# A planned attention and rational-FFN kernel: the first batch's sixteen units in another order, and a planner that tries five slacks

## The chip, the core and the metric

One core of one Trainium2 chip runs the kernel. The metric is the device time of one execution in microseconds. The kernel before takes 781.16 us, the median of three runs (780.78 to 782.17).

## The reference

For each of 8 batches and 8 heads, 32 packed queries `p` attend over 576 keys and values of width 64; then the 576 queries `q` attend over the 32 packed rows that came out. The result, 4608 tokens of 512 features, goes through a feed-forward layer with a rational activation:

```
p_packed = sm_attn(p, k, v)
x = sm_attn(q, p_packed, p_packed)          # 4608 x 512
h = x @ w_in                                # 512 -> 2048
P = a[0] + a[1]*h + a[2]*h^2 + a[3]*h^3
Q = 1 + |b[0]|*|h| + |b[1]|*h^2
out = (P / (Q + 1e-6)) @ w_out              # 2048 -> 512
```

The weights arrive as 64-bit floats and are taken apart by integer instructions on the chip.

## The kernel before

A batch `bb` has 576 tokens in two halves `x` of 288; the 2048 hidden features are eight chunks `c` of 256. A **unit** is one (batch, half, chunk), 128 in all, and the list `units` (L950) gives their order: batch by batch, in each batch the first half's eight chunks and then the second half's.

A unit runs in `hidden` (L876). TensorE makes `h` for two sets of 128 features in the two PSUM tiles of `h_ring`, so the tile of a unit's first set comes free when ScalarE has read it three times (into `Y`, `U`, `sq`) and VectorE twice (the two instructions that write `Y` from `h`). GpSimd adds `U` and `sq`, ScalarE takes the logarithm and exponential into `V` (which is in PSUM), VectorE makes `Y`, `V` and the product `g`. Three steps later `acc_block` (L955) multiplies 256 of the unit's tokens by rows of `w_out` into two PSUM tiles of `acc_ring`; the eight chunks of one half add up there, then ScalarE copies the sum out. The 32 tokens of a half that are left over are collected in `G` and multiplied by `remainder`. `m_chunk` folds `w_in` into the packed rows, one tile `M[bb, c // 2]` for two chunks.

The weights of the first batch come in while it runs. There are 16 words to convert, eight chunks of `w_in` (`in`) and eight of `w_out` (`out`). `convert` issues for each word two ScalarE passes and three VectorE passes (`tensor_scalar`, `scalar_tensor_tensor`, `tensor_add` on integers; the third is a custom instruction in the trace and `ISA` in the built order). `due` (L430) says at which unit a word is wanted and sorts the list; a word of `in` is due two units ahead of its chunk, one of `out` three units behind. `DIVIDE` later splits each chunk of `w_out` in a high and a low part (ScalarE copy, GpSimd subtractions). The first `PLAIN` = 12 units multiply undivided.

None of this is the order on the chip. Every instruction is recorded by `Planner` (L32), and `order` (L249) lists them anew. `schedule` (L191) is a list scheduler with one queue per engine, costs per instruction and a way time between engines; `order` runs it forward and backward in turn and ranks by the backward run's times, `ROUNDS` = 8 rounds, and the plan with the earliest end is kept. `SLACK` = 150 ns is added to each way in the backward run. `shares` (L136) says which VectorE instructions can't run beside a GpSimd one: in the plan, one waits until the other is done. `tensor_scalar`, `tensor_copy` and the integer `tensor_add` are such, if nothing in PSUM takes part; the `scalar_tensor_tensor` of a conversion is not. Where the plan leaves TensorE idle in the first 150 us, `idle` puts in small multiplications by `zero` (L285).

Of the kernel before, what the change touches and what calls it, by code (L numbers as in the profile page):

```python
# [31 lines left out]
class Planner:  # L32
# [8 lines left out]
    TRANSPOSE, F32 = (15, 0.734), (30, 1.62)  # L41
# [15 lines left out]
    WAY.update({("sync", x): 80 for x in ENGINES})  # L57
    PASS = 200
    FIRST = {"tensor": 700.0, "vector": 800.0, "scalar": 2000.0, "gpsimd": 1400.0, "sync": 700.0}
    ROUNDS = 8  # L60
    SWITCH = 95
    SLACK = 150
    IN_FLIGHT = 8
    DMA_ISSUE, DMA_START, DMA_END = 420, 1400, 1200

# [70 lines left out]
    def shares(self, engine, calls):  # L136

        if engine == "gpsimd":
            return True
        if engine != "vector":  # L140
            return False
        name, args, _ = calls[0]
        aps = [x for x in args if isinstance(x, bass.AP)]
        if any(x.space == PSUM for x in aps):
            return False
        return name in ("tensor_scalar", "tensor_copy") or (name == "tensor_add" and aps[0].dtype == I32)

    def mode(self, engine, calls):

# [38 lines left out]
            edges.append(before)  # L188
        return edges

    def schedule(self, before, after, rank, back=False):  # L191

        n = len(rank)
        need = [len(x) for x in before]
        at, start, end = [0.0] * n, [0.0] * n, [0.0] * n
        soon = {e: [] for e in self.ENGINES}
        ready = {e: [] for e in self.ENGINES}
        free = dict.fromkeys(self.ENGINES, 0.0) if back else dict(self.FIRST)
        port = {"vector": 0.0, "gpsimd": 0.0}
        mode, landed, dma = None, [], 0.0  # L200
        for i in range(n):
            if not need[i]:
                heapq.heappush(soon[self.ops[i][0]], (0.0, rank[i], i))
        now = 0.0
        left = n
        while left:
            for e in self.ENGINES:
                while soon[e] and soon[e][0][0] <= now:
                    heapq.heappush(ready[e], heapq.heappop(soon[e])[1:])
                if free[e] > now or not ready[e]:  # L210
                    continue
                if e == "sync" and not back and len(landed) >= self.IN_FLIGHT and landed[-self.IN_FLIGHT] > now:
                    free[e] = landed[-self.IN_FLIGHT]
                    continue
                _, i = heapq.heappop(ready[e])
                left -= 1
                s = now
                if e == "tensor" and not back and self.modes[i] != mode:
                    s += self.SWITCH
                    mode = self.modes[i]  # L220
                if not back and self.shared[i]:
                    s = max(s, port["vector" if e == "gpsimd" else "gpsimd"])
                    port[e] = s + self.costs[i]
                start[i] = s
                end[i] = free[e] = s + self.costs[i]
                if e == "sync":
                    if back:
                        dma = max(dma, end[i]) + self.transfers[i]
                        end[i] = dma + self.DMA_START + self.DMA_END - self.DMA_ISSUE
                    else:  # L230
                        dma = max(dma, s + self.DMA_START) + self.transfers[i]
                        end[i] = dma + self.DMA_END
                        landed.append(end[i])
                for j in after[i]:
                    need[j] -= 1
                    f = self.ops[j][0]
                    way = self.WAY.get((f, e) if back else (e, f), self.PASS)
                    way += self.SLACK * (back and way > 0)
                    at[j] = max(at[j], end[i] + way)
                    if not need[j]:  # L240
                        heapq.heappush(soon[f], (at[j], rank[j], j))
            now = min(
                t
                for e in self.ENGINES
                for t in ([free[e]] if ready[e] else [max(soon[e][0][0], free[e])] if soon[e] else [1e12])
            )
        return start, end

    def order(self):  # L249
        n = len(self.ops)  # L250
        self.costs = [self.price(*x) for x in self.ops]
        self.transfers = [self.transfer(calls[0][1]) if engine == "sync" else 0 for engine, calls in self.ops]
        self.shared = [self.shares(*x) for x in self.ops]
        self.modes = [self.mode(*x) for x in self.ops]
        before = self.edges()
        after = [[] for _ in range(n)]
        for i, x in enumerate(before):
            for j in x:
                after[j].append(i)
        rank = list(range(n))  # L260
        best = None
        for r in range(self.ROUNDS):
            start, end = self.schedule(before, after, rank)
            if best is None or max(end) < best[0]:
                best = self.best = max(end), start, end
            s, e = self.schedule(after, before, [-x for x in end], True)
            m = max(e)
            rank = [m - x for x in e]
            rank[: self.pinned] = range(-self.pinned, 0)
        self.end, self.start = best[0], best[1]  # L270
        self.deps, self.t0 = dict(enumerate(before)), best[1]
        return sorted(range(n), key=lambda i: (best[1][i], i))
# [47 lines left out]
def attention_rational_ffn(  # L320
# [27 lines left out]
    LAG = 3  # L348
# [78 lines left out]


    words = [(kind, 2 * c, 2) for kind in ("in", "out") for c in range(NCH)]
    due = lambda x: x[1] // 2 + (LAG if x[0] == "out" else -2)  # L430
    words.sort(key=due)
    index = {(kind, i): r for r, (kind, j, n) in enumerate(words) for i in range(j, j + n)}

# [440 lines left out]
    GS = {}  # L874

    def hidden(bb, x, c):  # L876
        plain = (2 * bb + x) * NCH + c < PLAIN
        mh, ml = (M[bb, c // 2][:, i, :, c % 2 * CF : (c % 2 + 1) * CF] for i in range(2))
        parts = [(mh, AH[bb])] if bb == 0 else [(mh, AH[bb]), (ml, AH[bb]), (mh, AL[bb])]
        U, V, Y = U_ring.next(), V_ring.next()[:, :, 0:HALF], Y_ring.next()  # L880
# [1 line left out]
        for f in range(2):  # L882
            h = h_ring.next()[:, 0:HALF]
            for i, (w, a) in enumerate(parts):
                for g in range(NG):
                    nc.tensor.matmul(
                        h, w[:, g, f * P : (f + 1) * P], a[:, g, x * HALF : (x + 1) * HALF],
                        start=g == 0 and i == 0, stop=g == NG - 1 and i == len(parts) - 1,
                    )
            u, y = U[:, f, :], Y[:, f, :]  # L890
            nc.scalar.activation(y, h, AF.Identity, scale=reg_a3, bias=a2)
            nc.scalar.activation(u, h, AF.Abs, scale=reg_b0)
# [11 lines left out]
        yield  # L904
        r0 = (bb % 2) * REM + x * HREM
        if plain:
            g = GS[bb, x, c] = (gh_ring if c % 2 == 0 else gl_ring).at(c // 2 % 2, dtype=F32)
# [40 lines left out]


    units = [(bb, x, c) for bb in range(B) for x in range(2) for c in range(NCH)]  # L950
    NU = len(units)
    UB = 2 * NCH
    ACC, O = {}, {}

    def acc_block(u, i):  # L955
        bb, x, c = units[u]
        if c == 0 and i == 0:
            ACC[bb, x] = [acc_ring.next() for _ in range(2)]
        acc = ACC[bb, x][i]
        cols = slice(i * P, (i + 1) * P)  # L960
        if u < PLAIN:
            for f in range(2):
                g = GS[bb, x, c][:, f, cols]
                nc.tensor.matmul(acc, g, X[c][:, f, :], start=c == 0 and f == 0, stop=c == NCH - 1 and f == 1)
        else:
            gh, gl = GS[bb, x, c]
        for f in range(0 if u < PLAIN else 2):
            accumulate(acc, gh[:, f, cols], gl[:, f, cols], 2 * c + f, c == 0 and f == 0, c == NCH - 1 and f == 1)
        if c < NCH - 1:
            return  # L970
        if i == 0:
            O[bb, x] = o_next()
# [2 lines left out]
        ov = out[bb * T : bb * T + NS * P, :].rearrange(order, i=2, x=2)[:, x]  # L975
        if u == NU - 1 and i == 1:
            nc.vector.tensor_copy(o[:, i, :], acc)
        else:
            nc.scalar.copy(o[:, i, :], acc)
        if u == NU - 1:  # L980
# [20 lines left out]
    STEPS = 16  # L1001
    mt, fill, rem = {}, {}, {}
    for c in range(1, NCH):
        mt[max(0, 2 * c - 3)] = 0, c
    for bb in range(1, B):
        for c in range(0, NCH, 2):
            mt[2 * UB * bb + 2 * c - 7] = bb, c, 2
# [95 lines left out]
```

## Time and profile before

| | |
|---|---|
| median of three runs | 781.16 us |
| the profiled execution, its own time | 780.48 us |
| its span, first to last instruction | 778.7 us |
| instructions | 15003 |
| TensorE / VectorE / ScalarE / GpSimd busy | 743.9 / 690.6 / 654.8 / 451.8 us |
| mean granted TensorE clock | 0.99 |

The profiled execution is 1.8 us longer than its span and 0.7 us shorter than the median. PE, DVE, ACT and POOL are TensorE, VectorE, ScalarE and GpSimd; PEld is TensorE's weight load. Nearly every instruction has the line of the planner's replay (L288; L285 for the idle ones), so groups are told apart by the tiles that they write and read: `h`, `acc`, `at` are PSUM tiles, `w`, `m`, `half`, `win` hold weights. Tiles change names as buffers are used again.

### The profile page before, as it was taken

Reading aid. Unit: us, or ns where it says so; the run is one execution under the profiler, and the core shown is the slowest. Engines: PE = TensorE matmul, PEld = TensorE weight load, DVE = VectorE, ACT = ScalarE, POOL = GpSimd, SP = SyncE. Lnnn points to the kernel's source line nnn. Section 1 sums busy time; section 2 is a strip of 40 time slices with the busy share of each in tenths; the row PEclk is TensorE's granted clock in tenths of the full one; section 3 lists DMA queues with packets and bytes.
Section 4 is the critical chain, followed back from the end, with each engine's and each line's share of the span. In section 5 each row is a group of like instructions: output and inputs, shape, how many; then the busy total and the mean of one; then the engine's idle time right before and its main releaser. Section 6 shows DMA issues by size and latency. Waiting matters only on the chain.

```text
span 778.7 us, 15003 instructions
## 1 busy us (share of the span) xinstructions
PE 743.9 (96%) x5350; PEld 569.8 (73%) x5350; DVE 690.6 (89%) x1295; ACT 654.8 (84%) x1464; POOL 451.8 (58%) x448
## 2 busy tenths in 40 slices
PE   2769999999999999999999999999999999999997
PEld 2435554678788787778788787778778787778886
DVE  4899999987998879998998889998999789998872
ACT  5889978998887988998897898998898798898881
POOL 0012357756695556765596556855586556856663
PEclk9979999999999999999999999999999999999999
DMA  9984260023601155022701128021801023000001
GB/s 299 369 272 145 103 122 28 1 86 53 105 1 55 45 60 98 1 86 38 120 1 55 45 38 120 1 64 41 112 27 55 34 46 40 14 12 17 28 0 42
DMA packets 152028, 56.04 MB, mean 72 GB/s; under 512 B 122256, under 2 KB 141200, under 8 KB 151952
## 3 DMA queue, kind: packets, MB, share of 16 engines
q1 hardware_dynamic: 151952, 55.07, 30.3%
q8 instruction: 42, 0.69, 0.4%
q14 instruction: 34, 0.28, 0.1%
HBM read 45.62 MB, written 9.44 MB: 71 GB/s over the span
## 4 chain that ended last, share of the span: by engine, by line
PE 71%; DVE 12%; ACT 11%; DMA 2%; issue 2%; POOL 1%; SPq 0%; DVEq 0%; ACTq 0%; POOLq 0%
PE acc L288 37%; PE h L288 22%; PE at L288 12%; DVE Y L288 4%; DVE w L288 2%; ACT V L288 2%; ACT Y L288 2%; DVE small L288 2%; DVE kx L288 2%; DMA nat<-in_k_dram 2%; ACT U L288 2%; ACT sq L288 1%; ACT half L288 1%; ACT w L288 1%; DVE V L288 1%
## 5 line engine op out<-in xcount | busy, mean ns | idle before, releaser
L288 POOL TENSOR_TENSOR U<-U,sq 128x576 f32<-128x576 f32 x128 | 184.9, 1444 | 102.1 <-ACT U L288 47.5
L288 PE MATMUL acc<-w,gh 128*128 128x512 f32 x736 | 236.9, 406 | 0.3
L288 PE MATMUL h<-AH,m 128*128 128x288 f32 x1024 | 200.6, 318 | 4.7 <-DVE Y L288 4.0
L288 PEld LDWEIGHTS h<-AH,m 128*128 128x128 f32 x1024 | 160.0, 189 | 45.8 <-DVE Y L288 24.5
L288 POOL TENSOR_TENSOR gl<-Y,gh 128x512 fp32r<-128x512 f32 x116 | 150.4, 1296 | 46.1 <-ACT gh L288 15.2
L288 PEld LDWEIGHTS acc<-w,gh 128*128 128x128 f32 x736 | 133.5, 188 | 44.0 <-issue 9.0
L288 ACT ACTIVATE Y<-h,abS 128x288 f32<-128x288 f32 x256 | 128.5, 518 | 25.0 <-PE h L288 20.1
L288 PE MATMUL acc<-w,gl 128*128 128x512 f32 x384 | 148.1, 412 | 0.2 <-DVE w L288 0.2
L288 ACT ACTIVATE sq<-h 128x288 f32<-128x288 f32 x256 | 108.9, 428 | 34.9 <-PE h L288 26.7
L288 DVE TENSOR_TENSOR Y<-Y,h 128x288 f32<-128x288 f32 x256 | 109.0, 444 | 26.7 <-ACT sq L288 11.6
L288 DVE SCALAR_TENSOR_TENSOR Y<-Y,abS,V 128x576 f32<-128x576 f32 x128 | 102.9, 804 | 27.5 <-ACT V L288 26.7
L288 DVE SCALAR_TENSOR_TENSOR Y<-Y,abS,h 128x288 f32<-128x288 f32 x256 | 124.7, 505 | 2.2
L288 ACT ACTIVATE U<-h 128x288 f32<-128x288 f32 x256 | 102.5, 432 | 11.2 <-DVE V L288 7.4
L288 ACT ACTIVATE V<-U,one 128x576 f32<-128x576 f32 x128 | 99.4, 777 | 10.8 <-DVE Y L288 7.9
L288 PE MATMUL h<-AL,m 128*128 128x288 f32 x448 | 96.0, 295 | 0.0
L288 DVE SCALAR_TENSOR_TENSOR V<-U,V 128x576 f32<-128x576 f32 x128 | 95.8, 749 | 0.0
L288 DVE SCALAR_TENSOR_TENSOR Y<-V,Y 128x576 f32<-128x576 f32 x116 | 86.3, 744 | 1.4
L288 PEld LDWEIGHTS acc<-w,gl 128*128 128x128 f32 x384 | 71.3, 188 | 20.1 <-issue 6.4
L288 ACT ACTIVATE V<-V 128x576 f32<-128x576 f32 x128 | 85.5, 668 | 0.4
L288 PE MATMUL acc<-half,gh 128*128 128x512 f32 x240 | 78.7, 409 | 0.0
L288 ACT CAST gh<-Y 128x512 fp32r<-128x512 f32 x116 | 73.7, 635 | 2.0 <-DVE Y L288 1.3
L288 PEld LDWEIGHTS h<-AL,m 128*128 128x128 f32 x448 | 71.8, 188 | 0.6 <-issue 0.5
(135 smaller groups left out, 955.5 us busy)
## 6 DMA issues: line engine op xcount, KB each, us to landing
w<-in_moe_w_out_dram SPq DMA_DIRECT2D x16, 512.0 KB, 4.4
out_dram<-half SPq DMA_DIRECT2D x15, 512.0 KB, 3.1
nat<-in_k_dram SPq DMA_DIRECT2D x48, 144.0 KB, 3.8
nat<-in_q_dram SPq DMA_DIRECT2D x48, 144.0 KB, 4.3
nat<-in_v_dram SPq DMA_DIRECT2D x24, 256.0 KB, 3.3
m<-in_moe_w_in_dram SPq DMA_DIRECT2D x8, 512.0 KB, 5.7
w<-in_moe_w_in_dram SPq DMA_DIRECT2D x8, 512.0 KB, 9.6
nat<-in_k_dram SPq DMA_DIRECT2D x4, 512.0 KB, 8.5
```

Of the source, the lines that this page charges most:

```text
L288: getattr(getattr(self.nc, engine), name)(*args, **kwargs)
```

## The change

The first batch's 16 units go in four groups of four: first half with chunks 0 to 3, second half with chunks 0 to 3, second half with chunks 4 to 7, first half with chunks 4 to 7. So chunks 4 to 7 are wanted from unit 8 on, not from unit 4 on, and `due` says so through `first`. The first half's sum is in two pieces: after chunk 3 ScalarE copies both tiles of `acc` into a buffer (`AL_ring`, not in use in the first batch), and after chunk 7 VectorE adds them to the second piece in place of ScalarE's copy. `PLAIN` counts by a unit's place in the list.

The planner takes any VectorE instruction with two inputs of over 8 columns (none in PSUM) for one that shares with GpSimd, which adds the conversions' `scalar_tensor_tensor` and, in the first batch's attention, the subtraction and multiplication on VectorE. It does six rounds from each of five slacks, and keeps the best of them.

```
-    ROUNDS = 8
+    ROUNDS = 6
-    SLACK = 150
+    SLACK = 60, 100, 150, 220, 300
...
-        return name in ("tensor_scalar", "tensor_copy") or (name == "tensor_add" and aps[0].dtype == I32)
+        wide = sum(self.columns(x) > 8 for x in aps[1:])
+        return wide > 1 or name in ("tensor_scalar", "tensor_copy")
...
-                    way += self.SLACK * (back and way > 0)
+                    way += back * (way > 0)
...
+        first = self.schedule(before, after, list(range(n)))
...
+        for slack in self.SLACK:
+            start, end = first
+            for r in range(self.ROUNDS):
+                s, e = self.schedule(after, before, [-x for x in end], slack)
...
+                start, end = self.schedule(before, after, rank)
+                if best is None or max(end) < best[0]:
+                    best = self.best = max(end), start, end
...
-    due = lambda x: x[1] // 2 + (LAG if x[0] == "out" else -2)
+    first = lambda c: c if c < NCH // 2 else c + NCH // 2
+    due = lambda x: first(x[1] // 2) + (LAG if x[0] == "out" else -2)
...
+    cut = NCH // 2
+    units[:2 * NCH] = [(0, x, y * cut + c) for x, y in ((0, 0), (1, 0), (1, 1), (0, 1)) for c in range(cut)]
...
+        if not whole:
+            return
         if c < NCH - 1:
+            if i == 0:
+                O[0] = AL_ring.at(0, dtype=F32)
+            nc.scalar.copy(O[0][:, i, 0:DM], acc)
             return
...
+        elif (bb, x) == (0, 0):
+            nc.vector.tensor_add(o[:, i, :], acc, O[0][:, i, 0:DM])
...
-    mt[max(0, 2 * c - 3)] = 0, c
+    mt[max(0, 2 * first(c) - 3)] = 0, c
```

Three places show what the planner makes of it.

The first is VectorE's queue just before unit 0. `AH0` is the attention's result for the first batch, which `h` needs; `w2` and `w4` hold raw words. Before:

```order
L288 STREAM_TRANSPOSE AH0_3_113<-kx0_1_87 128x576
L288 RECIPROCAL small_74<-small_74 128x18
L288 TENSOR_SCALAR w2_4_118<-w2_4_118 128x1024
L288 TENSOR_TENSOR kx0_1_87<-kx0_1_87,small_74 128x576
L288 SCALAR_TENSOR_TENSOR w2_4_118<-w2_4_118 128x1024
L288 STREAM_TRANSPOSE AH0_3_113<-kx0_1_87 128x576
L288 ISA win_72<-w4_6_120,win_72 128x2048
L288 ISA win_72<-w2_4_118,win_72 128x2048
```

The same stretch now:

```order
L291 STREAM_TRANSPOSE AH0_3_113<-kx0_1_87 128x576
L291 TENSOR_TENSOR kx0_1_87<-kx0_1_87,small_74 128x576
L291 TENSOR_SCALAR w2_4_118<-w2_4_118 128x1024
L291 STREAM_TRANSPOSE AH0_3_113<-kx0_1_87 128x576
L291 SCALAR_TENSOR_TENSOR w2_4_118<-w2_4_118 128x1024
L291 TENSOR_SCALAR w3_5_119<-w3_5_119 128x1024
L291 ISA w0_8_133<-w2_4_118,w0_8_133 128x2048
```

One conversion pass has gone from ahead of the second transpose to behind it, and the word in `w2` is now a chunk of `w_out` (its third pass writes `w0`, not `win`).

The second place is VectorE's queue where the last word is done. `V0_9` belongs to unit 8, the ninth. Before:

```order
L288 SCALAR_TENSOR_TENSOR w3_15_203<-w3_15_203 128x1024
L288 TENSOR_TENSOR Y0_10_245<-Y0_10_245,h0_19_247 128x288
L288 TENSOR_TENSOR Y0_10_245<-Y0_10_245,h1_20_251 128x288
L288 SCALAR_TENSOR_TENSOR Y0_10_245<-Y0_10_245,abS_68,h0_19_247 128x288
L288 SCALAR_TENSOR_TENSOR Y0_10_245<-Y0_10_245,abS_68,h1_20_251 128x288
L288 SCALAR_TENSOR_TENSOR Y2_9_228<-Y2_9_228,abS_68,V0_9_227 128x576
L288 ISA w5_17_236<-w3_15_203,w5_17_236 128x2048
L288 SCALAR_TENSOR_TENSOR V0_9_227<-U0_9_226,V0_9_227 128x2x288
```

Now the last word's second and third pass stand here, and `V0_12` is that of unit 11:

```order
L291 SCALAR_TENSOR_TENSOR w2_14_229<-w2_14_229 128x1024
...
L291 SCALAR_TENSOR_TENSOR Y2_12_271<-Y2_12_271,abS_68,V0_12_270 128x576
L291 RECIPROCAL small_74<-small_74 128x18
L291 ISA w5_16_266<-w2_14_229,w5_16_266 128x2048
L291 SCALAR_TENSOR_TENSOR V0_12_270<-U1_12_269,V0_12_270 128x2x288
```

The last word ends three units later. At units 8, 9 and 10 the queue has one second and one third pass less ahead of it than before (15 of 16 third passes); at unit 11 it has all of them.

The third place is TensorE's queue where `h` tiles follow each other closest outside the first batch. Before, at unit 108 (`h0_217`):

```order
L288 MATMUL h1_216_1330<-AH0_9_1129,m1_30_1187 128x288 x4
L288 MATMUL h1_216_1330<-AL0_6_1130,m1_30_1187 128x288 x2
L288 MATMUL acc0_37_1242<-w4_21_315,gl1_98_1310 128x512
L288 MATMUL acc1_38_1243<-w4_21_315,gl1_98_1311 128x512
...
L288 MATMUL h0_217_1337<-AH0_9_1129,m2_31_1208 128x288 x4
```

Now, at unit 116 (`h0_233`):

```order
L291 MATMUL h0_231_1409<-AH1_10_1308,m1_35_1363 128x288 x4
L291 MATMUL h0_231_1409<-AL1_8_1309,m1_35_1363 128x288 x2
L291 MATMUL h1_232_1412<-AH1_10_1308,m1_35_1363 128x288 x4
L291 MATMUL h1_232_1412<-AL1_8_1309,m1_35_1363 128x288 x2
L291 MATMUL acc0_41_1331<-w4_20_318,gl1_106_1392 128x512
L291 MATMUL acc1_42_1332<-w4_20_318,gl1_106_1392 128x512
L291 MATMUL h0_233_1419<-AH1_10_1308,m2_36_1382 128x288 x4
```

Between a pair of `h` tiles and the next pair in the same two buffers there are two multiplications now, where the closest pair before had these two and a set of small ones (left out above, `at<-kx,ppT`). Elsewhere the queues after the first batch are the same work in a somewhat different sequence. TensorE has 14 idle multiplications in the first batch where it had 19, and it enters a set of small tiled multiplications 73 times where it entered one 76 times.

More of the change, by code (lines that the diff above doesn't have):

```diff
@@ L189, in edges, with schedule @@
         return edges
-    def schedule(self, before, after, rank, back=False):
+    def schedule(self, before, after, rank, back=0):
         n = len(rank)
@@ L259, in order @@
                 after[j].append(i)
-        rank = list(range(n))
+        first = self.schedule(before, after, list(range(n)))
         best = None
[L262 to L269, printed above, removed]
+        for slack in self.SLACK:
+            start, end = first
+            for r in range(self.ROUNDS):
+                s, e = self.schedule(after, before, [-x for x in end], slack)
+                m = max(e)
+                rank = [m - x for x in e]
+                rank[: self.pinned] = range(-self.pinned, 0)
+                start, end = self.schedule(before, after, rank)
+                if best is None or max(end) < best[0]:
+                    best = self.best = max(end), start, end
         self.end, self.start = best[0], best[1]
@@ L876, in hidden @@
     def hidden(bb, x, c):
-        plain = (2 * bb + x) * NCH + c < PLAIN
+        u = units.index((bb, x, c))
+        plain = u < PLAIN
         mh, ml = (M[bb, c // 2][:, i, :, c % 2 * CF : (c % 2 + 1) * CF] for i in range(2))
@@ L889, in hidden @@
                     )
-            u, y = U[:, f, :], Y[:, f, :]
+            uf, y = U[:, f, :], Y[:, f, :]
             nc.scalar.activation(y, h, AF.Identity, scale=reg_a3, bias=a2)
-            nc.scalar.activation(u, h, AF.Abs, scale=reg_b0)
+            nc.scalar.activation(uf, h, AF.Abs, scale=reg_b0)
             nc.scalar.activation(U2[:, f, :], h, AF.Square, scale=reg_root)
@@ L906, in hidden @@
         if plain:
-            g = GS[bb, x, c] = (gh_ring if c % 2 == 0 else gl_ring).at(c // 2 % 2, dtype=F32)
+            g = GS[bb, x, c] = (gh_ring if u % 2 == 0 else gl_ring).at(u // 2 % 2, dtype=F32)
             for o, cols in ((g, slice(0, HMAIN)), (G[:, 2 * c : 2 * c + 2, r0 : r0 + HREM], slice(HMAIN, HALF))):
@@ L956, in acc_block @@
         bb, x, c = units[u]
-        if c == 0 and i == 0:
+        fresh, whole = c in ((0, cut) if (bb, x) == (0, 0) else (0,)), c in ((cut - 1, NCH - 1) if (bb, x) == (0, 0) else (NCH - 1,))
+        if fresh and i == 0:
             ACC[bb, x] = [acc_ring.next() for _ in range(2)]
@@ L963, in acc_block @@
                 g = GS[bb, x, c][:, f, cols]
-                nc.tensor.matmul(acc, g, X[c][:, f, :], start=c == 0 and f == 0, stop=c == NCH - 1 and f == 1)
+                nc.tensor.matmul(acc, g, X[c][:, f, :], start=fresh and f == 0, stop=whole and f == 1)
         else:
@@ L967, in acc_block @@
         for f in range(0 if u < PLAIN else 2):
-            accumulate(acc, gh[:, f, cols], gl[:, f, cols], 2 * c + f, c == 0 and f == 0, c == NCH - 1 and f == 1)
+            accumulate(acc, gh[:, f, cols], gl[:, f, cols], 2 * c + f, fresh and f == 0, whole and f == 1)
+        if not whole:
+            return
         if c < NCH - 1:
+            if i == 0:
+                O[0] = AL_ring.at(0, dtype=F32)
+            nc.scalar.copy(O[0][:, i, 0:DM], acc)
             return
```

## The prediction

> **What bounds the kernel now.** I read the page first. All lines below are of the kernel before.
>
> ```profile
> span 778.7 us, 15003 instructions
> PE 743.9 (96%) x5350; PEld 569.8 (73%) x5350; DVE 690.6 (89%) x1295; ACT 654.8 (84%) x1464; POOL 451.8 (58%) x448
> PE   2769999999999999999999999999999999999997
> DVE  4899999987998879998998889998999789998872
> ACT  5889978998887988998897898998898798898881
> ```
>
> PE is busy from the fourth slice to the last but one, and that is what a change has to shorten. But DVE reads 9 in slices 3 to 8, where the weights are converted, and a busy PE need not be a PE at its pace. So I cut the span by hand in windows (PE, PEld, DVE, ACT and POOL busy in each, then clock, DMA share, GB/s).
>
> ```profile
> 46.00:60.00 14.00, 11.10 (x62) 6.03 (x62) 13.13 (x21) 13.22 (x29) 3.11 (x3) 0.86 0.75 244
> 60.00:80.00 20.00, 20.00 (x140) 10.88 (x139) 19.58 (x33) 20.00 (x45) 5.34 (x4) 1.00 0.46 157
> 80.00:100.00 20.00, 19.91 (x177) 11.76 (x175) 19.95 (x42) 17.22 (x36) 7.20 (x5) 1.00 0.27 87
> 100.00:125.00 25.00, 24.67 (x116) 13.63 (x115) 25.00 (x47) 21.01 (x46) 17.91 (x13) 1.00 0.50 94
> 125.00:155.00 30.00, 29.59 (x153) 16.03 (x152) 29.10 (x58) 27.31 (x58) 22.05 (x20) 1.00 0.00 1
> 155.00:760.00 605.00, 601.31 (x4373) 483.89 (x4372) 546.17 (x1028) 520.61 (x1198) 389.09 (x393) 1.00 0.25 48
> ```
>
> Until 125 us DVE has no time left, from 125 to 155 it has 30.00 - 29.10 = 0.9 us, afterwards a tenth. PE is idle for 605.00 - 601.31 = 3.7 us in the whole long stretch, so hardly anything can be won there. The chain that ended last says where the bound passes from one engine to the next (start, length, what):
>
> ```profile
> 61.59 0.54 ACT V L288
> ...
> 82.61 1.05 ACT w L288
> ...
> 109.58 0.60 DVE w L288
> ...
> 124.25 0.79 DVE Y L288 x2
> ...
> 126.04 0.43 DVE Y L288
> 126.51 1.24 PE h L288 x4
> 127.75 0.86 PE acc L288 x2
> ```
>
> ACT until about 84 us, DVE until 126.5 us, PE from there to the end. What the change saves of DVE's work ahead of 126.5 us can arrive at the end, as long as PE can follow; what it saves behind it can't.
>
> **The change part by part.** First the conversions. The groups of DVE from 46 to 125 us (count, busy, mean ns of one), which hold ten units' `V`:
>
> ```profile
> L288 DVE SCALAR_TENSOR_TENSOR w<-w 128x1024 int32<-128x1024 int32 x9 | 11.8, 1315 | 0.0
> L288 DVE CUSTOM_DVE_ANT_0 w<-w,w 128x2048 uint16<-128x2048 uint16 x6 | 7.6, 1262 | 0.0
> L288 DVE SCALAR_TENSOR_TENSOR V<-U,V 128x576 f32<-128x576 f32 x10 | 7.5, 748 | 0.0
> ```
>
> All 16 words are still converted: the change moves, it doesn't remove. It also moves less than `due` suggests, since the planner ranks by its own backward run. In the built order one second pass and one third pass stand behind units 8, 9 and 10 that stood ahead of them: 1.3 + 1.3 = 2.6 us of a full DVE. By unit 11 they have been given back. The hand-over at 126.5 us lies just behind the tenth unit's `V`, so up to 2.6 us arrive. If PE then waits for DVE again at units 11 to 15, DVE can make good only its idle time there, 0.9 us. Bounds 0.9 and 2.6; I take the middle, 1.7 us gained, because PE already waits for nothing in most of that window (29.59 of 30.00).
>
> One of the second passes is the one that has gone behind the transpose into `AH0`; the first `h` can begin a pass, about 1.3 us, earlier. That is the same DVE work and no gain of its own: DVE is full up to 125 us and does it a little later. ScalarE's two passes and the DMA of a word move along; ACT has 20.00 - 17.22 = 2.8 us free in the window from 80 us, where they go, and the loads on SP are moved past each other while the DMA engines are busy for 0.27 of the time, so I cost both at nothing (if ACT had no room, two passes, some 2.5 us, would be late for the next unit). The `m_chunk` of chunks 4 to 7 goes with them, and PE needs them only from unit 8.
>
> Second, what passes take when they meet GpSimd. The instructions that touch `w` in that window (min/median/max ns):
>
> ```profile
> L288 DVE TENSOR_SCALAR w<-w x9: 679/689/1557, 48.4 to 109.5; 128x1024 int32<-128x1024 int32 x9
> L288 DVE SCALAR_TENSOR_TENSOR w<-w x9: 1214/1218/1595, 50.5 to 110.8; 128x1024 int32<-128x1024 int32 x9
> L288 POOL TENSOR_TENSOR w<-w,w x8: 1271/1283/2260, 102.6 to 123.4; 128x512 fp32r<-128x512 f32 x8
> L288 DVE CUSTOM_DVE_ANT_0 w<-w,w x6: 1204/1214/1369, 52.8 to 114.7; 128x2048 uint16<-128x2048 uint16 x6
> ```
>
> The second pass takes 1218 ns by its median and 1315 by its mean, 9 x 0.10 = 0.9 us in all over what it needs. Its cost in the plan was that of an instruction that meets nobody; the plan now counts it, and I take the 0.9 us as gained (bounds: none, and 0.9 lost if the later words meet more). The Trainium skill, "SBUF — State Buffer", section "Who interferes with whom", says that a DVE instruction with two SBUF inputs and a GpSimd instruction that reads SBUF take a shared port in turn, the later one blocked for the whole of the other. The maxima of the four rows agree with such a rule. By it each meeting costs up to a whole GpSimd instruction, and the sum would have a term for meetings, not for means; the rival on GpSimd below prices that.
>
> Third, PE behind the first batch. PE enters sets of small tiled multiplications 73 times in place of 76. An entry costs 0.33 us from start to start of its neighbours where a plain multiplication takes 0.23 (0.69 for three):
>
> ```profile
> 228.63 0.40 PE L288 MATMUL acc<-half,gl 128*128 128x512 f32 x1
> 228.86 0.62 PE L288 MATMUL acc<-half,gh 128*128 128x512 f32 x2
> 229.32 0.40 PE L288 MATMUL acc<-half,gl 128*128 128x512 f32 x1
> 229.65 1.09 PE L288 MATMUL at<-win,ppT 64*32 64x512 f32 x16
> ```
>
> Three entries by 0.10 us are 0.3 us gained. Against it stands the reuse of the `h` tiles. PE's waits for `h` tiles (total, times, longest), and the longest of them, at the closest pair of tiles:
>
> ```profile
> PE h L288 <- DVE Y L288: 4.0, 6, 1.3
> ```
>
> ```profile
> 655.96 0.43 PE L288 MATMUL h<-AL,m 128*128 128x288 f32 x2
> 656.22 0.63 PE L288 MATMUL acc<-w,gl 128*128 128x512 f32 x2
> 656.78 0.72 PE L288 MATMUL at<-kx,ppT 64*32 64x288 f32 x16
> 658.75 0.79 PE L288 MATMUL h<-AH,m 128*128 128x288 f32 x4 [1.26 <-DVE Y L288]
> ```
>
> The next pair started 658.75 - 656.39 = 2.4 us after the last one's end. In the changed order that place is mended, but at unit 116 only two multiplications, 0.5 us, stand between two pairs. By this row PE would wait 2.4 - 0.5 = 1.9 us there; at the least, a tile's own three instructions in a line (one ACT and two DVE, 0.5 us each by the rows below) less the second `h` of its pair (0.8) and the 0.5, some 0.2 us. With 1.26 us won back this is between 0.6 lost and 1.1 gained. The least has no queueing in it and the row has, so I stay near the row: 0.3 lost.
>
> Fourth, the first half's sum in two pieces: two ACT copies of `acc` more, and two DVE additions in place of two ACT copies. The same forms elsewhere:
>
> ```profile
> 772.67 0.59 ACT L288 COPY half<-acc 128x512 f32<-128x512 f32 x1 [5.78 <-PE at L288]
> 755.03 0.68 DVE L288 TENSOR_TENSOR full<-at,full 128x512 f32<-128x512 f32 x1
> 751.72 0.48 ACT L288 ACTIVATE Y<-h,abS 128x288 f32<-128x288 f32 x1
> 754.24 0.50 DVE L288 SCALAR_TENSOR_TENSOR Y<-Y,abS,h 128x288 f32<-128x288 f32 x1
> ```
>
> Two copies, 1.2 us, fall in the window from 80 us with ACT's 2.8 us free; two additions, 1.4 us, come behind 155 us, where DVE is busy for 546 of 605 us. Before the next `acc` can start, PE waits for a copy; PE has `h` tiles and an `m_chunk` between. I cost this at nothing (uncovered, 0.6 us a copy).
>
> The sum: -1.7 - 0.9 - 0.3 + 0.3 = -2.6 us. The profiled execution's own 780.48 becomes 777.9 and the median of 781.16 becomes 778.6. A measurement of this kernel can tell 0.2%, 1.56 us, from no change: faster is below 779.6, slower above 782.7.
>
> **The rivals.**
>
> *Given back.* DVE is full to 125 us and 29.10 of 30.00 to 155 us, and every word is done by unit 11. Then only 0.9 us of the 1.7 arrive, the passes meet GpSimd as before, and unit 116 costs its full 0.6: -0.9 - 0.3 + 0.6 = -0.6, 780.6 us. For it: the planner leaves nearly as much DVE work ahead of unit 15 as before. Against it: the chain has left DVE by then. Chance 0.31.
>
> *The last words meet GpSimd.* GpSimd subtracts the split weights from 102.6 us on, and the change moves the last three words, nine DVE passes, towards that time. If each waits half of the worst that a first pass shows, (1557 - 689) / 2 = 0.43 us, DVE loses 3.9 us while it is the bound, none of the 0.9 is won, and PE stands still behind it: -1.7 - 0.3 + 0.3 + 3.9 = +2.2, 783.4 us. It decides when the meetings cost DVE over 3.3 us more than before. Against it: GpSimd's subtractions are queued later too, and GpSimd is busy for 17.91 of 25.00 us there already. Chance 0.16. The Trainium skill, "SBUF — State Buffer", section "Who interferes with whom", would have it so wherever the two engines' instructions start side by side; the maxima above agree, the medians show that most don't meet.
>
> *The idle time closes.* PE's idle time is 2.9 us from 46 to 60, 0.8 from 60 to 155, 3.7 behind it; these rows of idle multiplications add 4.4:
>
> ```profile
> L285 PE MATMUL acc<-half,zero 128*64 128x96 f32 x20 | 2.3, 254 | 0.0
> L285 PE MATMUL acc<-w,zero 128*64 128x96 f32 x18 | 2.1, 254 | 0.0
> ```
>
> The new plan has 14 such multiplications for 19, so it expects less idling. Half of the 11.8 us gained would be 775.3 us. Against it: until 126.5 us PE's idling is not the bound. Chance 0.05.
>
> **How the numbers follow.** The forecast has 0.48; its own range is 777.7, where DVE's two terms have their better ends (2.6 + 0.9, PE's two cancelling), to 779.6. Faster is the forecast and the last rival, 0.53; given back is within 0.2%, 0.31; the words that meet GpSimd are slower, 0.16. The range takes in *given back* with the whole band of no change and reaches down to the last rival's time: 775.0 to 782.8, which leaves out the 0.16 and a little of the 0.05.
>
> **What would show it.** In the changed kernel's chain the last DVE piece before PE takes over for good should end about 2 us before 126.5; if it ends later, and DVE is full to 155, it was given back. The second pass's mean over `w` should be near 1.22 us. PE's waits for DVE's `Y` behind 155 us should still add up to some 3 us, with one at unit 116. I am wrong if the saving stands behind 155 us, or if the first `h` begins no earlier and the time falls all the same.

## The result and the profile after

The changed kernel takes 776.98 us (774.46 to 780.77), the kernel before 781.12 (779.72 to 782.44), both medians of 20 runs in turn on one chip: a ratio of 0.995 (95% interval 0.9939 to 0.996), 4.1 us faster. The forecast was 2.6 us faster, 778.6 in a range of 775.0 to 782.8. The number came out; of its reasons only a part did, and some 2 us stand in a stretch that had no term in the sum. One later run of the changed kernel (in e5) took 1215.21 us at a mean granted clock of 0.56 and is left out of e5's median below.

The profiled execution of the changed kernel took 774.46, its fastest run, so its own 6.0 us of gain hold about 2 us of luck. The replay's line has moved from 288 to 291 (idle multiplications from 285 to 288), and in the experiments it lies between 288 and 300. First the page of the changed kernel:

```profile
span 772.7 us, 14982 instructions
PE 737.6 (95%) x5339; PEld 568.3 (74%) x5339; DVE 688.3 (89%) x1297; ACT 652.9 (85%) x1464; POOL 451.2 (58%) x448
```

The windows of the prediction from 60 to 760 us, of the changed kernel:

```profile
60.00:80.00 20.00, 19.95 (x179) 12.31 (x182) 19.97 (x41) 19.86 (x42) 4.63 (x4) 1.00 0.17 57
80.00:100.00 20.00, 19.31 (x108) 10.80 (x108) 19.91 (x39) 19.15 (x42) 7.40 (x5) 1.00 0.70 192
100.00:125.00 25.00, 25.00 (x144) 12.15 (x143) 24.92 (x45) 20.04 (x44) 13.46 (x11) 1.00 0.17 24
125.00:155.00 30.00, 29.78 (x151) 17.87 (x152) 29.23 (x57) 27.27 (x59) 24.08 (x21) 1.00 0.17 53
155.00:760.00 605.00, 600.92 (x4379) 486.23 (x4378) 545.96 (x1030) 519.08 (x1194) 393.05 (x395) 1.00 0.25 47
```

DVE is as full up to 125 us as it was. The chain of the changed kernel looks quite different, though:

```profile
64.00 1.20 ACT kx L291 x4
...
84.96 0.67 DVE V L291
86.61 1.16 DVE Y L291 x3
87.82 0.75 PE h L291 x2
89.17 1.65 PE h L291 x6
```

It leaves DVE at 87.8 us, where the chain of before left it at 126.5 (in e5, the same plan, at 89.6). By the reading that I used for before (the bound ends where the chain passes to PE) DVE would now be no bound behind 88 us. The experiments e7 and e8 show that this reading is wrong.

The three conversion passes on VectorE from 46 to 145 us, changed kernel (count, busy, mean ns):

```profile
L291 DVE SCALAR_TENSOR_TENSOR w<-w 128x1024 int32<-128x1024 int32 x9 | 11.7, 1302 | 0.0
L291 DVE CUSTOM_DVE_ANT_0 w<-w,w 128x2048 uint16<-128x2048 uint16 x5 | 6.1, 1217 | 0.0
L291 DVE TENSOR_SCALAR w<-w 128x1024 int32<-128x1024 int32 x8 | 5.5, 689 | 0.0
```

The second pass has not come down to 1.22 us. The last third pass now begins at 128.5 us (114.7 before):

```profile
L291 DVE CUSTOM_DVE_ANT_0 w<-w,w x5: 1167/1221/1256, 46.6 to 128.5; 128x2048 uint16<-128x2048 uint16 x5
```

To see where the time went I cut both traces where ScalarE begins the logarithm (`V<-U,one`) of a unit, and asked for the windows between. The kernel before, from unit 16's to unit 112's logarithm and from there to the end:

```profile
159.20:689.20 530.00, 526.31 (x3956) 421.90 (x3955) 481.25 (x913) 455.54 (x1050) 340.78 (x344) 1.00 0.28 52
689.20:778.70 89.50, 85.41 (x458) 70.09 (x456) 65.72 (x116) 65.55 (x148) 51.76 (x52) 0.99 0.06 22
```

The changed kernel:

```profile
156.20:682.90 526.70, 524.40 (x3950) 421.21 (x3937) 481.48 (x916) 455.06 (x1050) 343.10 (x346) 1.00 0.29 51
682.90:772.70 89.80, 83.28 (x443) 70.29 (x441) 65.29 (x114) 64.54 (x146) 51.70 (x52) 0.99 0.06 21
```

So 3.0 us had been won by unit 16, another 3.2 between units 16 and 112 (530.0 and 526.8 before the windows' rounding), and nothing behind. The middle number is the surprise: the first stage's conversions have nothing to do there, and PE had only 3.7 us of idle time. PE's waits in the changed kernel from 155 us on (total, times, longest):

```profile
PE h L291 <- DVE Y L291: 3.4, 4, 1.8
PE acc L291 <- ACT half L291: 0.3, 2, 0.2
PE at L291 <- DVE kx L291: 0.2, 1, 0.2
```

The 1.8 us is at unit 116, where the prediction had put it.

### The profile page after: what moved, and what is told of

Read it like the earlier page. It is cut to its first block, busy times and chain, and to the rows that moved or that the text cites. A ratio compares the mean times of both kernels' runs of the same rounds, so it can differ in the third digit from the quotient of the medians.

```text
span 772.7 us, 14982 instructions
## 1 busy us (share of the span) xinstructions
PE 737.6 (95%) x5339; PEld 568.3 (74%) x5339; DVE 688.3 (89%) x1297; ACT 652.9 (85%) x1464; POOL 451.2 (58%) x448
## 3 DMA queue, kind: packets, MB, share of 16 engines
q1 hardware_dynamic: 151952, 55.07, 30.9%
## 4 chain that ended last, share of the span: by engine, by line
PE 72%; ACT 10%; DVE 10%; DMA 4%; POOL 1%; issue 1%; SPq 1%; DVEq 0%; POOLq 0%; ACTq 0%
PE acc L291 37%; PE h L291 22%; PE at L291 12%; DVE Y L291 5%; ACT Y L291 2%; DMA m<-in_moe_w_in_dram 2%; ACT V L291 2%; ACT sq L291 2%; ACT U L291 1%; DMA w<-in_moe_w_out_dram 1%; DVE m L291 1%; DVE V L291 1%; DMA w<-in_q_dram 1%; ACT kx L291 1%; ACT w L291 1%
## 5 line engine op out<-in xcount | busy, mean ns | idle before, releaser
L291 PE MATMUL h<-AH,m 128*128 128x288 f32 x1024 | 197.5, 316 | 4.2 <-DVE Y L291 4.1
L291 PE MATMUL acc<-w,gl 128*128 128x512 f32 x384 | 149.9, 413 | 0.0
L291 DVE TENSOR_TENSOR Y<-Y,h 128x288 f32<-128x288 f32 x256 | 110.6, 448 | 22.5 <-ACT sq L291 11.3
```

The costliest lines, as they stand in the source:

```text
L291: getattr(getattr(self.nc, engine), name)(*args, **kwargs)
```

## The experiments

The change has three parts: the **units'** order (with its due dates), the **slacks** of the search, the **sharing** rule. The search of the changed kernel ends up with slack 60. This table gathers all plans of the three parts, with the begin of unit 16's logarithm, the stretch from there to unit 112's, and the rest, each from one profiled execution (us). The kernel before beside them took 781.12 (changed), 781.57 (e1 to e4), 781.05 (e5 to e8) and 781.57 (e9 to e12). Two profiles of one plan agree within 0.2 us in the stretch (within 0.5 where e7 and e8, below, are taken in), but differ by up to 2.4 at unit 16: the first 60 us differ from execution to execution.

| kernel | units | slack | sharing | median | ratio to before (95%) | unit 16 | 16 to 112 | 112 to end |
|---|---|---|---|---|---|---|---|---|
| before | old | 150 | old | 781.12 | 1 | 159.2 | 530.0 | 89.5 |
| changed | new | 60 (found) | new | 776.98 | 0.995 (0.9939 to 0.996) | 156.2 | 526.8 | 89.7 |
| e5, the same | new | 60 (found) | new | 777.52 | 0.9955 (0.9942 to 0.9968) | 158.3 | 526.7 | 91.3 |
| e1 | new | 150 | old | 779.45 | 0.9974 (0.996 to 0.9987) | 160.6 | 529.7 | 89.5 |
| e2 | old | searched | new | 781.66 | 1.0004 (0.9988 to 1.0019) | 160.2 | 531.9 | 88.8 |
| e3 | new | 60 (found) | old | 775.25 | 0.9935 (0.9913 to 0.9957) | 157.5 | 528.0 | 88.0 |
| e4 | new | 150 | new | 779.07 | 0.9967 (0.9953 to 0.9982) | 159.4 | 529.5 | 89.2 |
| e6 | new | 300 | new | 784.80 | 1.0047 (1.0035 to 1.006) | 162.9 | 530.2 | 90.5 |
| e9 | old | 60 | old | 780.08 | 0.9981 (0.997 to 0.9993) | 159.2 | 530.4 | 88.1 |
| e10 | new | 100 | old | 780.31 | 0.9989 (0.9977 to 1.0001) | 161.4 | 529.4 | 88.8 |
| e11, as e3 | new | 60 (found) | old | 775.53 | 0.9927 (0.9913 to 0.9941) | 157.7 | 527.8 | 88.0 |

**The parts, one and two at a time: e1 to e4.** e1 takes the new units and the planner of before; e2 the old units and the new planner:

```
 e1:
-    SLACK = 60, 100, 150, 220, 300
+    SLACK = 150
...
-        wide = sum(self.columns(x) > 8 for x in aps[1:])
-        return wide > 1 or name in ("tensor_scalar", "tensor_copy")
+        return name in ("tensor_scalar", "tensor_copy") or (name == "tensor_add" and aps[0].dtype == I32)
 e2:
-    units[:2 * NCH] = [(0, x, y * cut + c) for x, y in ((0, 0), (1, 0), (1, 1), (0, 1)) for c in range(cut)]
```

and with these lines all else that goes with them (before's search of eight rounds in e1; due dates, halves of the sum and `PLAIN` in e2).

> The new order of the units with the old planner (one slack of 150 ns, the old rule on sharing with GpSimd). In its built order 15 of 16 third passes stand ahead of unit 8's V, and 15 until unit 11, as in the full change. Theory A (the units' order takes a conversion from ahead of VectorE's hand-over): 2 to 3 us faster than before, and in the profile unit 10's logarithm comes 2 us or more earlier than 124.1 us. Theory B (all comes from the planner): within 1 us of before.

> The old order of the units with the new planner (new rule on sharing, five slacks, six rounds each). All 16 third passes stand ahead of unit 8's V, as before. Theory A: 0 to 1.5 us faster, from behind 155 us, with unit 10 not earlier than 123 us. Theory B: 4 us faster, as the full change.

e3 is the changed kernel with the old sharing rule alone (the lower half of e1's edit), e4 the changed kernel with the one slack alone (its upper half).

> The full change without the new rule on sharing: conversions' second passes are again taken for ones that meet nobody. Theory A with a gain from the rule: 1 us slower than the full change, some 3 us faster than before. Theory B with the rule as the main part: no faster than before. If the rule does nothing: as the full change, 4 us faster than before.

> The full change without the five slacks (one of 150 ns, eight rounds). Theory A: 2 to 3.5 us faster than before. Theory B with the search over slacks as the main part: within 1 us of before.

The units alone are worth 2.1 us (e1 against the 781.57 beside it), the new planner alone nothing (e2). With the units, the sharing rule adds nothing that can be told (779.07 for 779.45), and the search does: e3 is 6.3 us faster than the kernel before beside it, and faster than the whole change by its median. Most of the gain of the steady stretch comes with the search: 528.0 in e3, 529.5 and 529.7 without it, 530.0 before. The sign that I had named for e1, unit 10's logarithm 2 us earlier than 124.1, did not come: it stands at 124.2 in e1's profile. But there the granted clock was 0.50 from 42 to 58.8 us and the first logarithm came at 55.0 for 51.0, so this profile neither shows the sign nor refutes it.

**The changed kernel again, and a slack that moves more: e5 and e6.** e5 is the changed kernel but for a comment; e6 has

```
-    SLACK = 60, 100, 150, 220, 300
+    SLACK = (300,)
```

and by that plan two third passes fewer than before stand ahead of units 8 to 11, not one.

> The changed kernel unchanged, for a second profile and times on the chip of the next three runs. Time 777.0, 4 to 5 us faster than before. In its profile VectorE leaves the chain before 110 us, as in the first profile (87.8 us, against 126.5 before); from unit 16's to unit 112's logarithm 526.8 us plus or minus 0.7, against 530.0 before, if that difference belongs to the plan and not to the single execution.

> The full change with the one slack of 300 ns. Its order puts off the most conversions: 14 of 16 third passes ahead of units 8 to 11, where the full change has 15 and before 16. Theory A (VectorE's work ahead of the hand-over sets the gain): unit 15's logarithm no later than in the full change, 148 to 150 us. Theory B (the plan behind the first batch sets it): unit 15 as in before, about 153 us, and the total differs by what happens behind it.

e5 repeats the steady stretch to 0.1 us: it belongs to the plan. e6 overthrows the simple form of my first step. More passes were moved back, and it is slower than before by 3.7 us. Its windows:

```profile
100.00:125.00 25.00, 25.00 (x150) 12.78 (x150) 25.00 (x44) 20.97 (x47) 5.76 (x5) 1.00 0.50 82
125.00:155.00 30.00, 30.00 (x167) 18.35 (x166) 29.63 (x53) 23.64 (x49) 25.60 (x20) 1.00 0.01 3
```

DVE is full to 155 us with what was postponed. From unit 0's logarithm to unit 8's it took 60.1 us (before 60.2), from there to unit 16's 50.0 (before 48.0): nothing gained and 2.0 given back. That is the rival that I called *given back*, in a sister of the changed kernel.

**Is VectorE the bound of the first stage, and how far? e7 and e8.** In the kernel before (e7) and in the changed one (e8) the first VectorE pass of the last six words is issued four times in place of once, in the same plan. It writes the same value again.

```
+                extra = engine == "vector" and name == "tensor_scalar" and args[2] == -0x80000000
+                passes = passes + 1 if extra else passes
+                for _ in range(4 if extra and passes > 10 else 1):
...
```

> Before, with the first VectorE pass of the last six words done four times (18 more passes of 0.69 us, 12.4 us of VectorE work, same order otherwise; the result of a pass doesn't change when it is done again). They stand ahead of units 2 to 8. Theory A (VectorE is the bound until 126 us): 9 to 12.4 us slower. Rival (TensorE is the bound from 60 us on and VectorE's full slices are cover): under 4 us slower.

> The changed kernel with the same 18 more passes for the last six words, here ahead of units 3 to 11. Theory A: VectorE has left the chain at 88 us in this kernel, so 2 to 5 us less of the 12.4 arrive than in the kernel before. Rival: as much slower as the kernel before is by the same passes.

e7 took 800.17 us, 19.1 more (ratio 1.0247, 1.0234 to 1.026), e8 794.85, 17.3 more than e5 beside it (to before 1.018, 1.0164 to 1.0196). That is more than 18 passes of 689 ns, and more than the 12.4 us that were expected of e7 at most. The group in e7, from 46 to 145 us, shows why:

```profile
L291 DVE TENSOR_SCALAR w<-w 128x1024 int32<-128x1024 int32 x27 | 23.6, 875 | 0.6
```

The group was 9 by 783 ns, 7.1 us; it is 23.6 now, and the eleven third passes in that window take 15.7 us for 13.6. So 16.5 + 2.1 = 18.6 us of DVE work were added, and 19.1 arrived. In e8 the group went from 8 passes and 5.5 us to 26 and 22.1: 16.6 added, 17.3 arrived. Four of the six words, two thirds of what was added, begin behind 96 us, and 5.7 us of the delay came between unit 8's and unit 16's logarithm (54.7 for 49.0 in e5), though the chain had left DVE at 88 us in that plan. e8's chain leaves it 45 us later:

```profile
101.38 1.78 DVE w L294
...
127.87 1.63 DVE w L294
129.50 0.67 DVE V L294
...
131.65 1.14 DVE Y L294 x3
132.83 3.74 PE h L294 x8
```

A part of what arrived can be lost clock. TensorE now waits longer in places, and behind such waits the granted clock was at 0.50 for 3.4 us, three times in e8 (from 78.7, 106.0 and 133.3 us) and twice in e7 (from 99.9 and 120.3); in the kernel before and the changed one it was 1.00 throughout from 60 to 155 us. At half the clock 3.4 us cost at most 1.7, so of the 17.3 us at least 12 and of the 19.1 at least 15 came without it (estimates from these figures). So DVE bounds the first stage of both kernels to beyond unit 8, or is so near to it that most of every added microsecond arrives. A chain that passes to PE earlier says only that PE was at least as late there.

**Is it the slack, or slack and units together? e9 and e10.** e9 is the kernel before with `SLACK = 60`; e10 is e3 with `SLACK = (100,)`.

> The kernel before with SLACK = 60 in place of 150 and nothing else: old order of units, old sharing rule, the search's chosen slack. Theory A (the 2 us that the search won lie in how slack 60 orders the steady stretch, whatever the first units are): from unit 16's logarithm to unit 112's about 527 to 528.5 us where before took 530.0, and 778 to 779.5 us in all. Theory B (slack 60 is worth something only beside the new order of units): 529.5 us or more in that stretch and 780.5 to 782 us in all.

> The new order of units with the old sharing rule and one slack of 100 that the search did not choose. Theory A (the gain of the steady stretch belongs to slack 60's plan alone): 529 to 530.5 us from unit 16 to unit 112 and 778.5 to 780 us in all, as with slack 150. Theory B (every smaller slack wins there): 527 to 528.5 us and 775 to 777.5 us.

e9's and e10's steady stretches:

```profile
159.20:689.60 530.40, 527.84 (x3974) 422.88 (x3973) 482.08 (x917) 455.92 (x1051) 342.49 (x344) 1.00 0.29 52
```

```profile
161.40:690.80 529.40, 525.51 (x3930) 418.68 (x3931) 480.72 (x914) 454.71 (x1048) 341.81 (x342) 1.00 0.28 51
```

Neither has the gain of the steady stretch (e9 is 1.5 us faster than before; its profile has 1.4 of that behind unit 112). In e9 theory A fell, in e10 theory B, and each time lies 0.3 to 0.4 us outside the range of the theory that is left. Slack 60 with the old units gives 530.4, the new units with another slack 529.4, only both together 526.7 to 528.0. The steady stretch's 2 to 3 us are no property of one part; they are what one plan happens to have.

**The sharing rule's price: e11.** This is e3 once more.

> The changed kernel with the old sharing rule, once more. If the new sharing rule really costs a little: 775 to 776.5 us again, ratio to before 0.991 to 0.9945. If the earlier 775.25 was the luck of one run: 777 to 778.5 us, ratio 0.995 to 0.997. From unit 16 to unit 112 some 528 us in both cases.

775.53 us: no luck of one run. The changed kernel without its sharing rule is the fastest of all these, 6.0 and 6.3 us ahead of the kernel before beside it where the whole change is 4.1 and 3.5 ahead. Its second pass is longer all the same:

```profile
L290 DVE SCALAR_TENSOR_TENSOR w<-w 128x1024 int32<-128x1024 int32 x9 | 12.7, 1418 | 0.0
```

And its waits from 155 us on hold no long one:

```profile
PE h L290 <- DVE Y L290: 1.6, 3, 0.7
PE acc L290 <- ACT gh L290: 0.4, 1, 0.4
```

**The wait at unit 116: e12.** In the changed kernel's plan, unit 116's two `h` tiles are put four `acc` multiplications later; a few of ScalarE's reads of `h` change places with each other.

```
+        late = max(key[j] for j in pair) + 1000
+        for i in range(n):
+            key[i] = max([key[i], late * (i in pair), *(key[j] for j in before[i])])
...
```

> The changed kernel, but unit 116's two h tiles stand four acc multiplications later in TensorE's queue, so that VectorE has 0.9 us more to read the tiles before them; nothing else moves but three ScalarE reads. If the wait there is VectorE's and costs what it shows: the wait of 1.95 us falls to about 1.0 and the time from unit 112's logarithm to the end from 89.7 to about 88.8, 776.5 to 777.5 us in all. If it is made up for behind (rival): the wait falls and the end comes no sooner, 777.0 to 778.5 us.

778.56 us (0.9963, 0.9949 to 0.9977): not faster, and not by either theory. (The expectation's 1.95 us for the wait is 1.8 in the traces.) PE's waits from 685 to 705 us in e12, and in e5, which has the pair unparted:

```profile
PE acc L300 <- ACT half L300: 3.2, 1, 3.2
```

```profile
PE h L291 <- DVE Y L291: 1.8, 1, 1.8
```

The four multiplications begin a new sum. Their `acc` tile is free only when ScalarE has copied the last sum out, and that copy stands behind six reads of `h`, a logarithm, a cast and an exponential in ScalarE's queue. A wait of 1.8 for VectorE became one of 3.2 for ScalarE: two queues are late at this place, not one. From unit 112's logarithm to the end it takes 93.7 us in e12, 91.3 in e5, 89.7 in the changed kernel's first profile and 88.0 in e3 and e11, which have the same units and slack, the old sharing rule and no such wait. The changed kernel's 1.8 us reach the end nearly whole by this, 1.7 of them; where e5 and e12 lost more, the granted clock was lower (last section). The kernel before takes 89.5 there.

## Why the prediction was right, and where it was wrong

**What bounds the kernel: the reading of the chain was wrong twice.** I wrote "PE from there to the end" for the chain of before behind 126.5 us, from a few lines of it. The page of that profile says otherwise:

```profile
PE 71%; DVE 12%; ACT 11%; DMA 2%; issue 2%; POOL 1%; SPq 0%; DVEq 0%; ACTq 0%; POOLq 0%
```

What is not PE is 29% of 778.7, 226 us, and only 126.5 us lie ahead of the hand-over. Between 155 and 760 us the chain has 497 us of PE, 54 of ACT, 33 of DVE, 7 of DMA and 6 of GpSimd. The other error was to take the end of DVE's last piece for the time when DVE stops being the bound, which e8 refutes. The sign built on it, that piece 2 us earlier, was useless: it moved by 39.

**Step one, conversions behind units 8 to 10, 1.7 us of 0.9 to 2.6: a gain of that size stands ahead of unit 16, but not at these units.** From unit 0's logarithm to unit 8's the three profiles of this plan (changed, e5, e12) take 57.2, 57.5 and 58.4 us where before took 60.2; from there to unit 16's each takes 49.0 for 48.0. That leaves 2.0, 1.7 and 0.7, and unit 16's logarithm stands at 156.2, 158.3 and 158.6 for 159.2. Cut at VectorE's own instruction, the one that writes `V` from `U`, the places come out differently. From unit 0's logarithm to unit 0's `V` the plan takes 3.3 us where before takes 5.5 (e7, which is the same up to there, 4.9): 7 third and 8 first passes stand ahead of that `V`, not 8 and 9. From unit 0's `V` to unit 8's it takes 57.3, 57.9 and 58.8 for 59.4, from there to unit 16's 48.2, 48.0 and 48.0 for 45.6. So what the later units win is given back by unit 16, as the rival *given back* had it, and what is kept stands at unit 0, where I had counted the passes that move as no gain. I had also misread the built order: at unit 10 only a third pass is still behind, since the last second pass (119.6 us) stands ahead of its `V` (122.7).

How much of this the units' order alone does is open. e1 and e4, the new units without the search, are 2.1 and 2.5 us faster, but e4, with as many third passes ahead of units 8 to 11 as the changed kernel, takes 108.5 us from unit 0's logarithm to unit 16's (before 108.2), e10 takes 109.5, and e2 and e9, which have the old units, 105.3 and 105.6. e6 gained nothing there. The count of passes behind a unit doesn't settle it alone, and single profiles of one plan differ by more than a microsecond there.

**Step two, the second pass spared GpSimd, 0.9 us: failed.** I had written that the plan now counts this pass and so its mean falls to 1.22 us. It is 1302 ns (1315 before). The passes did become shorter, elsewhere: the first from 783 to 689 ns, the third from 1262 to 1217. The three means add up to 3.21 us a word for 3.36, nine times 0.15 = 1.4 us. But e3 and e11, with the old rule, pay 3.37 and 3.34 a word and are faster, and with slack 150 the rule changes nothing (3.28 with it in e4, 3.29 without in e1). The second pass with the largest excess, 1827 ns where the median is 1223, begins at 119.60 us while a GpSimd addition runs until 120.34: 0.74 us are left of that addition, and the pass is 0.60 us longer. The rule of the Trainium skill, "SBUF — State Buffer", section "Who interferes with whom", fits this; that a planner which knows the rule makes a faster kernel is not what these runs show.

**Step three, three entries into tiled sets fewer, 0.3 us:** nothing here resolves it.

**The two copies and two additions, nothing:** they don't show in the chain quoted above; in e8's the two copies take 1.0 us. No run here tells them apart.

**Step four, the `h` tiles, 0.3 us lost: the places and the waits were right, the price a little low.** The row-based estimate was 1.9 us at unit 116, and the wait is 1.8; the 1.26 us at unit 108 went, as I had counted on. Together that is 0.5 lost. I had let a lower bound without queueing shrink it to 0.3. Of the 1.8, 1.7 arrive beside e3 and e11 (88.0 us from unit 112's logarithm to the end, 89.7 here).

**The step that was missing: the long stretch from 155 us.** I wrote that hardly anything can be won there. Between units 16 and 112 it gave 3.2 us, in each of the three profiles of this plan. PE's idle time fell from 530.00 - 526.31 = 3.7 to 526.70 - 524.40 = 2.3, which is 1.4 us, and most of that is the wait at unit 108, 1.26, which step four had counted. The other 1.9 us are PE time that counts as busy, and nothing in the sum stood for them. Of the whole, 2.1 us stand where a group of `h` follows a multiplication into `acc`: 124 such places take 33.0 us from start to start before, 126 take 30.9 now. A search over whole plans re-deals these places everywhere. Which pairs of places make up the rest is open, since some records are missing in each trace. Behind unit 112, too, there is something that I had not forecast: e3 and e11 take 1.5 us less there than before (88.0 for 89.5), and in the changed kernel this hides the wait.

So, against the profile of before: some 1.5 us forecast and found ahead of unit 16 (the mean of three profiles, from 0.6 to 3.0), though at another unit; 0.9 forecast and not found; 0.5 lost at the `h` tiles for a forecast 0.3; 1.9 in the long stretch and 1.5 behind it not forecast. That the sum fell within 1.5 us of the measured 4.1 is in good part luck: what was not found and what was not forecast cancel. Both of my own conditions for being wrong are met: a good half of the saving stands behind 155 us, and the first `h` began at 43.2, 45.0 and 44.2 us (changed, e5, e12) for 44.0 before, so in e5 and e12 no earlier, and the time fell all the same. Of the rivals, *given back* had the mechanism between units 8 and 16 right and the time wrong; *the idle time closes* had 1.4 us in the long stretch, most of it at unit 108; *the last words meet GpSimd* did not happen, with the first pass at 689 ns.

## What to carry to other kernels

Where a planner orders a whole program, an edit of one stage and a number in the planner act together, and on every stage: the same new units and rule were worth from 4.1 us gained (slack 60) to 3.7 lost (slack 300) by the slack alone, so several plans are to be run on the chip, and the price of a wait is to be looked up in the plan that comes out. The hand-over in a chain of waits (read in full, not in a few lines) shows who was last, not how far the others are behind; to learn whether an engine bounds a stage, give it a known piece of work more and see how much arrives. A wait at a close pair of tiles is to be costed in full where the engine that waits is the bound, and every queue that releases it looked at, before it is moved.

## What was not expected of the hardware

Behind the wait of 1.8 us TensorE's granted clock was lower in one execution and not in others. The windows around unit 116's wait in the changed kernel's first profile and in e5's, where the wait is the same (the last three columns are clock, DMA share, GB/s):

```profile
692.00:702.00 10.00, 8.63 (x47) 7.62 (x48) 9.21 (x17) 9.50 (x23) 6.30 (x8) 1.00 0.14 52
```

```profile
685.00:695.00 10.00, 8.75 (x59) 6.49 (x58) 9.13 (x18) 9.29 (x22) 6.00 (x7) 1.00 0.01 2
695.00:705.00 10.00, 9.48 (x44) 8.21 (x45) 7.80 (x15) 8.00 (x20) 5.51 (x6) 0.83 0.14 52
```

In e12, behind its wait of 3.2 us:

```profile
693.00:697.00 4.00, 0.92 (x6) 0.48 (x4) 3.91 (x8) 4.00 (x11) 2.23 (x3) 0.89 0.00 0
697.00:707.00 10.00, 9.86 (x42) 8.80 (x43) 5.57 (x10) 5.79 (x15) 3.62 (x4) 0.70 0.14 52
```

The granted clock was 1.00 in one execution behind the wait and 0.83 over 10 us in another; the second took 1.5 us longer to the end, all of it between the logarithms of units 112 and 116 (20.1 for 18.6). Cut finer, e5's loss is one piece at half the clock:

```profile
697.20:700.60 3.40, 3.40 (x11) 2.73 (x10) 3.21 (x7) 2.83 (x8) 1.95 (x3) 0.50 0.41 154
```

In e12 it is 0.50 from 696.2 to 703.0 us, and in e8, whose wait at unit 116 is 1.8 as well, it stayed at 1.00. Over all fourteen traces, from 61 us on and leaving out the last 10 us, the clock was at half seven times, each time beginning during a wait of TensorE or within 3 us of its end: behind all six waits of 2.4 us or more (2.4, 2.6, 2.9, 3.2, 4.2 and 4.6, in e7, e8 and e12), and behind one of the fourteen waits of 1.0 to 1.8 us, e5's. So in these traces a wait of 2.4 us or more cost more than itself, up to another 1.7 us for each 3.4 us at half the clock (an estimate: half of 3.4).

The Trainium skill, "TensorE: Matmul & The Clock Gate", Part 1, has the gate fall back to half the clock after an idle window of about 3.4 us that runs freely. The pieces at half the clock agree, with 3.4 us or twice that in every case, but the idle time ahead of them was as short as 2.4 us, and once 1.8; here the measurement differs from the page. Why one wait of 1.8 us was followed by the lower clock and two of the same length (the changed kernel's and e8's) were not is open.
